# Finer TensorE blocks, one head-sum form, the root's product on GpSimd and an early exponential in a pre-norm attention and gMLP kernel

## The chip, the cores and the metric

The kernel runs on one core of one Trainium2 chip. The metric is device time in microseconds. The kernel before takes 737.69 us, the median of three runs (737.46 to 737.92).

## The reference

The input x has 2048 rows of 1024 features. Two residual blocks follow each other, each behind a layer norm without gain or offset.

```python
def _A_ref(x, wqkv, wo):            # 32 heads of 32
    W, dil = (8, 2)
    q, k, v = split heads of x @ wqkv
    idx = pos[:, None] - arange(W)[None, :] * dil
    logits = einsum('bhsd,bhswd->bhsw', q, k[idx]) * Dh ** -0.5, masked where idx < 0
    o = einsum('bhsw,bhswd->bhsd', softmax(logits), v[idx])
    return o @ wo

def _B_ref(x, w_in, w_sp, b_sp, w_out):   # F = 3584, Fh = 1792
    z = gelu(x @ w_in)
    z1 = z[..., :Fh]; z2 = layernorm(z[..., Fh:])
    g = einsum('ts,bsf->btf', w_sp, z2) + b_sp[None, :, None]
    return (z1 * g) @ w_out

h   = x + _A_ref(layernorm(x), ...)
out = h + _B_ref(layernorm(h), ...)
```

(The lines of `_A_ref` are shortened.) Attention looks at eight positions, two apart, so its logits are eight elementwise products of q with a shifted k, summed over the 32 features of a head. The spatial product with `w_sp` needs z2 of all rows, so it cannot start before the whole first part is through.

## The kernel before

Rows are worked in four chunks of 512 (four tiles of 128 rows). The kernel has two stages.

**The second stage**, from 442.6 us on, is plain: for each chunk the spatial product (L773), bias and gate on VectorE (DVE), and the output projection (L788). The change does not touch it.

**The first stage** is a list of operations that is put in order by a small planner at build time, the class `Order`. Each operation has an engine, an estimated duration, dependencies with a latency (0.1 us unless another is given), a priority (lower first), and slots that it takes or frees: three accumulators of two PSUM banks each ("acc"), one PSUM tile for logits ("L"), two product buffers and two partial-sum buffers. The planner keeps a clock for each engine. It picks the engine whose next operation can start first; among the operations of that engine that can start within 0.02 us of that, the lowest priority goes. It also keeps in mind which function table ScalarE (ACT) has loaded and adds 1.28 us where an operation names another one. The result is the order of instructions in the queues of TensorE (PE), ACT, DVE and GpSimd (POOL); on the chip each engine then works through its queue in that order and waits where data is not there yet. The DMAs issued by SP and POOL are put where the planner's time for them falls.

The operations that the change speaks of:

- `qkv(c)` (L351) projects chunk c to q, k and v: 12 accumulators per chunk, each two halves of eight matmuls of 512 columns (1.727 us planned). `b_z2(c)` (L627) and `b_z1(c)` (L677) are the two halves of the gMLP's input projection, `head(c)` (L554) is the attention's output projection. All of them split an accumulator in two halves, and the second depends on the first with the usual latency. ACT empties the accumulators (L363, L358 for q, k, v; L634 and L683 with gelu), for `head` DVE does it while adding the residual (L563).
- `attention(c)` on DVE: for each of eight window positions a product of q and shifted k for all heads (L407, 128x4096), then one add that halves the eight slices of 512 to four (L411). With `LMODE` 2 a second add halves them again to two (L414); with `LMODE` 4 it stops there. TensorE sums the rest of a head's features with a matmul against a 0/1 matrix of 32 columns (L430): in mode 2 two groups, each for four windows and of 8 matmuls with 512 columns, in mode 4 four groups, each for two windows and of 16 matmuls with 256 columns. Chunks 0 and 1 use mode 2, chunks 2 and 3 mode 4. Then the softmax: maximum and subtraction on DVE (L439, L447), exponential on ACT (L449), sums, reciprocal and product on DVE (L453 to L471), the spread over the features on TensorE (L483) and its copies to SBUF (L488), and eight multiplies and seven adds with v on DVE (L501, L504, L510), which end in the attention output oT of the chunk.
- `batch_rstd` computes mean, variance and reciprocal root for the layer norms of h ("l2", after `head`) and of z2 ("l3", after `b_z2`): four small operations on DVE, the root as a power of -0.5 on GpSimd (L524), then on DVE nb = -mean * rstd (L529). ACT then normalises in place with scale rstd and bias nb (L596 for l2 of chunks 0 to 2, L656 for l3 of chunks 0 to 2). Chunk 3's l2 is done per tile with one column and without nb, and DVE normalises (L580); chunk 3's l3 is normalised on DVE too (L658).

TensorE's queue in the first stage mixes these: `qkv(1..3)` runs beside the attention of chunks 0 and 1, `b_z2` and `b_z1` of chunks 0 to 2 beside the attention of chunks 2 and 3, and `head(c)` comes when oT of chunk c is done. `b_z1(2)` is split around `head(3)`; `b_z2(3)` and `b_z1(3)` end the stage. The transposed, normalised h (hnT) comes by DMA transposes from SP's queue (L586, L601).

Of the kernel before, what the change touches and what calls it, by code (L numbers as in the profile page):

```python
# [20 lines left out]
P = 128  # L21
# [10 lines left out]
NEG = -1.0e9  # L32
NWARM = 14
XRB = 2
LMODE = (2, 2, 4, 4)
LSLACK, BSLACK = 2.0, 2.0
Z2ACT = (4, 4, 4, 0)
LNPRIO = (0, 2.0, 2.5, 4.0)
LAST_COLS = ((0, 512), (512, 768), (768, 1024))

# [84 lines left out]
def kernel(  # L125
# [34 lines left out]
    maskb = csb[0:32, 288:416].rearrange("p (w s) -> p w s", w=W_WIN)  # L160
    eps_t = cpool.tile([P, 1], FP32, name="eps_t")
    V.memset(eps_t[:], EPS)
    nhalf = cpool.tile([P, TPC], FP32, name="nhalf")
    V.memset(nhalf[:], -0.5)
    mv1 = cpool.tile([P, NT, 2], FP32, name="mv1")
# [163 lines left out]
    def qkv(c):  # L329
        for xi in range(3):  # L330
            wv = wsb[xi][:].rearrange("p kt (m dl) -> p kt dl m", dl=DLO)
            for dp in range(DLO // 2):
                key = ("acc", "qkv", c, xi, dp)
                deps = [G.get(("xnT", c))]
                if c == 0 and xi == 0 and dp < 2:
                    def mm(wv=wv, dp=dp):
                        if dp == 0:
                            accs = [new_acc(), new_acc()]
                            G["acc", "qkv", 0, 0, 0], G["acc", "qkv", 0, 0, 1] = accs
                            for kt in range(KT):  # L340
                                for dl in range(4):
                                    T.matmul(accs[dl // 2][:, dl % 2, :], wv[:, kt, dl, :], xnT[0][:, kt, :],  # L342
                                             start=(kt == 0), stop=(kt == KT - 1))
                    last = add("PE", 6.91 if dp == 0 else 0.0, mm, deps, prio=order(), take="acc")
                else:
                    for j in range(2):
                        def mm(j=j, dl=2 * dp + j, wv=wv, key=key):
                            if j == 0:
                                G[key] = new_acc()
                            for kt in range(KT):  # L350
                                T.matmul(G[key][:, j, :], wv[:, kt, dl, :], xnT[c][:, kt, :],  # L351
                                         start=(kt == 0), stop=(kt == KT - 1))
                        last = add("PE", 1.727, mm, deps, prio=order(), take="acc" if j == 0 else None)
                        deps = [last]
                def ev(xi=xi, dp=dp, key=key):
                    if c == 0:
                        off = 0 if xi == 0 else HALO
                        A.copy(att_in[0][xi][:, 2 * dp:2 * dp + 2, off:off + CH], G[key][:])  # L358
                        if xi > 0 and dp == 3:
                            dma(qkv_d[xi][:, :, CH - HALO:CH], att_in[0][xi][:, :, CH:CH + HALO])  # L360
                    else:
                        stg = l1.tile([P, 2, CH], BF16, name="stg", tag="xn", bufs=4)
                        A.copy(stg[:], G[key][:])  # L363
                        dma(qkv_d[xi][:, 2 * dp:2 * dp + 2, c * CH:(c + 1) * CH], stg[:])
# [9 lines left out]
    def attention(c):  # L374
# [66 lines left out]
            st["ssum"] = att.tile([P, 4, P], FP32, name="ssum", tag="ssum")  # L441
        prev = add("DVE", 1.18, mx, lms, prio=3.0, take="prod")
        exps = []
        for hw in range(2):
            ws = slice(4 * hw, 4 * hw + 4)
            def sub(ws=ws):
                V.tensor_tensor(st["sme"][:, 0, ws, :], st["L"][:, ws, :], st["m"][:].unsqueeze(1).to_broadcast([P, 4, P]), op=ALU.subtract)  # L447
            prev = add("DVE", 0.61, sub, [prev], prio=3.0, lat=0.1, free="L" if hw == 1 else None)
            exps.append(add("ACT", 0.6, lambda ws=ws: A.activation(st["sme"][:, 1, ws, :], st["sme"][:, 0, ws, :], ACTF.Exp, scale=SCALE),  # L449
                            [prev], prio=0.0, table="exp"))  # L450
# [62 lines left out]


    def batch_rstd(key, sums, sqs, n, pfx, deps, prio, cols=TPC):
        def a1():
            t = {k: bp.tile([P, cols], FP32, name=pfx + k, tag=pfx + k) for k in ("mean", "msq", "var", "rstd", "nb")}
            G[key] = t
            V.tensor_scalar(t["mean"][:], sums(), 1.0 / n, None, op0=ALU.mult)
            V.tensor_tensor(t["msq"][:], t["mean"][:], t["mean"][:], op=ALU.mult)  # L520
            V.scalar_tensor_tensor(t["var"][:], sqs(), 1.0 / n, t["msq"][:], op0=ALU.mult, op1=ALU.subtract)
            V.tensor_scalar(t["var"][:], t["var"][:], 0.0, EPS, op0=ALU.max, op1=ALU.add)
        s1 = add("DVE", 0.74, a1, deps, prio=prio)
        s2 = add("POOL", 1.05, lambda: nc.gpsimd.tensor_tensor(G[key]["rstd"][:], G[key]["var"][:], nhalf[:, 0:cols], op=ALU.pow), [s1], lat=0.4)  # L524
        if cols < TPC:
            return s2
        def a3():
            t = G[key]
            V.scalar_tensor_tensor(t["nb"][:], t["mean"][:], -1.0, t["rstd"][:], op0=ALU.mult, op1=ALU.mult)  # L529
        return add("DVE", 0.16, a3, [s2], prio=prio)  # L530

    def head(c):
        last = c == NCH - 1
# [5 lines left out]
        for il in range(TPC):  # L539
            i = c * TPC + il  # L540
            deps = [G["avdone", c]]
            for half in range(2):
                def mm(half=half, il=il, i=i):
                    if half == 0:
                        if il == 0:
                            st["hsum"] = bp.tile([P, TPC], FP32, name="hsum", tag="hsum")
                            st["hsq"] = bp.tile([P, TPC], FP32, name="hsq", tag="hsq")
# [1 line left out]
                            for k in range(min(XRB, TPC)):  # L549
                                xr_load(k)  # L550
                        st["acc", il] = new_acc()
                    for dl in range(4 * half, 4 * half + 4):
                        for nh in range(2):
                            T.matmul(st["acc", il][:, nh, :], oTs[c][:, dl, il * P:(il + 1) * P], wo_sb[:, dl, nh * CH:(nh + 1) * CH],  # L554
                                     start=(dl == 0), stop=(dl == DLO - 1))
                def xr_load(k):
                    st["xr", k] = bp.tile([P, D], BF16, name="xr", tag="xr", bufs=XRB)
                    dma(st["xr", k][:], x2d[(c * TPC + k) * P:(c * TPC + k + 1) * P, :])
                m_ = add("PE", 1.727, mm, deps, prio=prio + il * 1e-2 + half * 1e-3, take="acc" if half == 0 else None)
                deps = [m_]  # L560
            def res(il=il, i=i):
                hb = st["hnc"][:, il, :]
                V.scalar_tensor_tensor(hb, st["acc", il][:].rearrange("p a b -> p (a b)"), 1.0, st["xr", il][:],  # L563
# [9 lines left out]
        if last:  # L573
            G["close"] = dma_op(0.0, close_, [G["headmm", c]] + [G["z2n", k, il] for k in range(c) for il in range(TPC)])
            for il in range(TPC):
                rs = batch_rstd(("l2", c, il), lambda il=il: st["hsum"][:, il:il + 1], lambda il=il: st["hsq"][:, il:il + 1],
                                D, f"l2_{il}", [sqd[il]], 0.5, cols=1)
                def nrm(il=il):
                    t = G["l2", c, il]
                    V.tensor_scalar(st["hnc"][:, il, :], st["hnc"][:, il, :], t["mean"][:], t["rstd"][:],  # L580
                                    op0=ALU.subtract, op1=ALU.mult)
                n_ = add("DVE", 0.5, nrm, [rs], prio=0.6)
                def tr(il=il):
                    if il == 0:
# [23 lines left out]
    def b_z2(c):  # L608
        st = {}
        sqd = []  # L610
        for il in range(TPC):
            evs = []
            for hf in range(2):
                wd = win_specs[hf][1]
                deps = [G.get(("hnT", c, il), G["hnT", c]), G["win", hf]]
                for half in range(2):
                    def mm(half=half, hf=hf, il=il, wd=wd):
                        if half == 0:
# [5 lines left out]
                        for kt in range(4 * half, 4 * half + 4):  # L624
                            for n0 in range(0, wd, CH):
                                n1 = min(n0 + CH, wd)
                                T.matmul(accf[:, n0:n1], hnTs[c][:, il, kt, :], wins[hf][:, kt, n0:n1],  # L627
                                         start=(kt == 0), stop=(kt == KT - 1))
                    m_ = add("PE", 1.727 if hf == 0 else 1.3, mm, deps, prio=order(), take="acc" if half == 0 else None)
                    deps = [m_]  # L630
# [19 lines left out]
        for il in range(TPC):  # L650
            i = c * TPC + il
            def nrm(il=il, i=i):
# [2 lines left out]
                if Z2ACT[c] > il:  # L655
                    A.activation(z2[:], st["u", il][:], ACTF.Identity, scale=t["rstd"][:, il:il + 1], bias=t["nb"][:, il:il + 1])  # L656
                else:
                    V.tensor_scalar(z2[:], st["u", il][:], t["mean"][:, il:il + 1], t["rstd"][:, il:il + 1], op0=ALU.subtract, op1=ALU.mult)  # L658
# [8 lines left out]
    def b_z1(c):  # L667
        for fp in range(NF // 2):
            deps = [G["hnT", c], G["win", 2 if fp < 4 else 3]]
            for j in range(2):  # L670
                def mm(j=j, fp=fp):
                    f = 2 * fp + j
                    wt, f0 = (wins[2], f) if f < 8 else (wins[3], f - 8)
                    if j == 0:
                        G["accy", c, fp] = new_acc()
                    for kt in range(KT):
                        T.matmul(G["accy", c, fp][:, j, :].rearrange("p (a b) -> p a b", a=TPC), wt[:, kt, f0 * P:(f0 + 1) * P],  # L677
                                 hnTs[c][:, :, kt, :], start=(kt == 0), stop=(kt == KT - 1))
                m_ = add("PE", 1.727, mm, deps, prio=order(), take="acc" if j == 0 else None)
                deps = [m_]  # L680
            def ev(fp=fp):
                z1s = l1.tile([P, 2, CH], BF16, name="z1s", tag="xn", bufs=4)
                A.activation(z1s[:], G["accy", c, fp][:], ACTF.Gelu_apprx_tanh)  # L683
# [150 lines left out]
```

## Time and profile before

| what | value |
|---|---|
| median of three runs | 737.69 us (737.46 to 737.92) |
| the profiled execution: its own time, its span | 737.65 us, 735.9 us |
| mean granted TensorE clock | 0.998 |
| attention outputs done on DVE, chunk 3 | 368.1 us |
| second stage begins | 442.6 us |
| ACT table loads: at L256, L449, L634, L683 | 1, 3, 1, 2 |
| GpSimd roots: L299, l2, l3, l2 of chunk 3 | 3, 3, 4, 4 |

The span runs from the first to the last instruction of one profiled execution; that execution's own time is 1.75 us longer. A row of a group gives the line, the engine, the operation, its tiles and shapes and its count, then the busy time of the group in us and the mean ns of one, then the idle time of the engine just before such an instruction and what ended it. Matmuls are pipelined, so the mean ns of one (379 for 512 columns) is longer than the spacing of two (0.216 us); a group's busy time counts the overlap once. DVE instructions in a row overlap by 0.08 us. A wait's row names engine, line and tile, what it waited for, and us in total, times and the longest. A row of the stages gives the window, its length, and busy time and instruction count of PE, PE's weight loads, DVE, ACT and POOL, then granted clock, DMA share and GB/s.

### The profile page before, as it was taken

The numbers are of one execution on the slowest core, as the hardware profiler recorded it, in microseconds if no ns is written. First come the engines' busy times: TensorE is split into PE (matmuls) and PEld (weight loads), VectorE is DVE, ScalarE is ACT, GpSimd is POOL, SyncE is SP. The second block draws the span as 40 slices with busy tenths as digits, with TensorE's granted clock in tenths as the row PEclk, the third lists the DMA queues.
The fourth block names the chain that finished last, engine by engine and source line by source line (L and its number), as shares of the span: only waits on it lengthen the run. The fifth ranks groups of instructions, "written<-read, shape, count | busy, mean of one in ns | idle before, by whom it ended". The sixth has DMA issues, their size and how long they took to land.

```text
span 735.9 us, 8608 instructions
## 1 busy us (share of the span) xinstructions
PE 725.7 (99%) x3580; PEld 369.1 (50%) x3580; DVE 416.8 (57%) x431; ACT 219.2 (30%) x267; POOL 50.0 (7%) x59
## 2 busy tenths in 40 slices
PE   7999999999999999999999999999999999999998
PEld 4666665566645444444444544444444444444444
DVE  4899899988999899889940012221232223212322
ACT  4322532534338954696563620000000000000000
POOL 0310200100102100300113000000000000000000
PEclk9999999999999999999999999999999999999999
DMA  9874563485484632370079988135104410020002
GB/s 337 315 242 116 191 184 122 153 231 200 149 324 109 210 113 74 115 227 18 29 229 338 256 243 268 40 95 148 58 29 112 133 57 31 28 86 29 1 15 71
DMA packets 113223, 105.27 MB, mean 143 GB/s; under 512 B 67776, under 2 KB 91744, under 8 KB 113056
## 3 DMA queue, kind: packets, MB, share of 16 engines
q1 hardware_dynamic: 105472, 72.63, 33.0%
q0 software_dynamic: 7280, 31.50, 12.1%
q8 instruction: 28, 0.46, 0.3%
q10 hardware_dynamic: 432, 0.59, 0.2%
q14 instruction: 11, 0.09, 0.0%
HBM read 55.09 MB, written 33.88 MB: 121 GB/s over the span
## 4 chain that ended last, share of the span: by engine, by line
PE 89%; DVE 7%; ACT 1%; POOL 1%; issue 1%; DMA 0%; POOLq 0%; DVEq 0%; ACTq 0%
PE acc L773 26%; PE acc L351 22%; PE acc L788 13%; PE acc L627 10%; PE acc L677 9%; PE acc L554 8%; DVE prod L504 2%; DVE oT L510 2%; PE acc L342 1%; DVE part L411 1%; POOL l3rstd L524 1%; PE L L430 1%; DMA xp<-in_A_x_dram 0%; PE tpa L252 0%; ACT z1s L683 0%
## 5 line engine op out<-in xcount | busy, mean ns | idle before, releaser
L773 PE MATMUL acc<-wspT,z2sb 128*128 128x512 bf16 x896 | 194.0, 379 | 0.0
L773 PEld LDWEIGHTS <-z2sb 128*128 128x128 bf16 x896 | 87.7, 98 | 105.7
L776 DVE TENSOR_TENSOR g<-acc,bB 128x1024 bf16<-128x1024 f32 x28 | 34.3, 1224 | 157.6 <-PE acc L773 133.0
L677 PE MATMUL acc<-hnT,win 128*128 128x512 bf16 x448 | 99.4, 379 | 0.5 <-ACT z1s L683 0.5
L627 PE MATMUL acc<-win,hnT 128*128 128x512 bf16 (+1 forms) x512 | 99.3, 352 | 0.0
L627 PEld LDWEIGHTS <-hnT 128*128 128x128 bf16 x512 | 49.8, 98 | 47.7 <-issue 0.9
L407 DVE TENSOR_TENSOR prod<-qT,kT 128x4096 bf16<-128x4096 bf16 x32 | 72.0, 2284 | 1.6 <-ACT kT L358 1.6
L788 PEld LDWEIGHTS <-zg 128*128 128x128 bf16 x462 | 45.2, 98 | 51.7
L677 PEld LDWEIGHTS <-win 128*128 128x128 bf16 x448 | 43.4, 98 | 52.5 <-issue 1.7
L504 DVE TENSOR_TENSOR prod<-vT,AB 128x4096 bf16<-128x4096 bf16 x28 | 63.8, 2289 | 1.0
L510 DVE TENSOR_TENSOR oT<-oT,prod 128x4096 bf16<-128x4096 bf16 x28 | 64.0, 2284 | 0.1
L363 ACT CAST stg<-acc 128x1024 bf16<-128x1024 f32 x36 | 36.4, 1011 | 78.6 <-PE acc L351 75.5
L788 PE MATMUL acc<-wout_a,zg 128*128 128x512 bf16 (+1 forms) x264 | 58.2, 373 | 0.0
L795 DVE TENSOR_TENSOR ot<-acc,hr 128x1024 bf16<-128x1024 f32 x15 | 18.4, 1224 | 69.4 <-PE acc L788 69.4
L351 PE MATMUL acc<-xnT,wv 128*128 128x512 bf16 x256 | 57.1, 380 | 0.0
L351 PE MATMUL acc<-xnT,wk 128*128 128x512 bf16 x256 | 57.1, 380 | 0.0
L554 PE MATMUL acc<-wo_sb,oT 128*128 128x512 bf16 x256 | 56.3, 379 | 0.7 <-DVE oT L510 0.7
L351 PE MATMUL acc<-xnT,wq 128*128 128x512 bf16 x224 | 49.8, 379 | 0.0
L351 PEld LDWEIGHTS <-wk 128*128 128x128 bf16 x256 | 36.4, 143 | 19.1 <-issue 0.9
L351 PEld LDWEIGHTS <-wv 128*128 128x128 bf16 x256 | 36.4, 143 | 19.1 <-issue 0.9
L788 PE MATMUL acc<-wout_b,zg 128*128 128x512 bf16 (+1 forms) x198 | 44.4, 373 | 0.0
L351 PEld LDWEIGHTS <-wq 128*128 128x128 bf16 x224 | 31.9, 143 | 16.8 <-issue 0.8
(125 smaller groups left out, 489.9 us busy)
## 6 DMA issues: line engine op xcount, KB each, us to landing
qkv_d<-stg SPq DMA_DIRECT2D x36, 256.0 KB, 2.5
z_d<-z1s SPq DMA_DIRECT2D x28, 256.0 KB, 2.6
z1c<-z_d SPq DMA_DIRECT2D x28, 256.0 KB, 2.7
z_d<-u SPq DMA_DIRECT2D x12, 448.0 KB, 2.9
z2sb<-z_d POOLq DMA_DIRECT2D x12, 448.0 KB, 9.2
xr<-in_A_x_dram SPq DMA_DIRECT2D x16, 256.0 KB, 2.8
h_d<-hb SPq DMA_DIRECT2D x16, 256.0 KB, 2.4
win<-in_B_w_in_dram POOLq DMA_DIRECT2D x2, 2048.0 KB, 9.1
```

The lines of the kernel that those rows point to most:

```text
L351: T.matmul(G[key][:, j, :], wv[:, kt, dl, :], xnT[c][:, kt, :], start=(kt == 0), stop=(kt == KT - 1))
L363: A.copy(stg[:], G[key][:])
L407: V.tensor_tensor(st["prod"][:], qT[:], kT[:, :, o:o + CH], op=ALU.mult)
L504: V.tensor_tensor(pvs[w][:], vT[:, :, o:o + CH], abb, op=ALU.mult)
L510: prev = add("DVE", 2.3, lambda w=w: V.tensor_tensor(oTs[c][:], oTs[c][:], pvs[w][:], op=ALU.add), [prev, m_], prio=3.0, lat=0.15, free="p ...
L554: T.matmul(st["acc", il][:, nh, :], oTs[c][:, dl, il * P:(il + 1) * P], wo_sb[:, dl, nh * CH:(nh + 1) * CH], start=(dl == 0), stop=(dl == ...
L627: T.matmul(accf[:, n0:n1], hnTs[c][:, il, kt, :], wins[hf][:, kt, n0:n1], start=(kt == 0), stop=(kt == KT - 1))
L677: T.matmul(G["accy", c, fp][:, j, :].rearrange("p (a b) -> p a b", a=TPC), wt[:, kt, f0 * P:(f0 + 1) * P], hnTs[c][:, :, kt, :], start=(kt ...
L773: T.matmul(acc[:, j, :], z2sb[a][:, f * P:(f + 1) * P], wspT[:, a, :], start=(a == 0), stop=(a == NT - 1))
L776: V.tensor_tensor(g1[:], acc[:], bB[:, c * CH:(c + 1) * CH].unsqueeze(1).to_broadcast([P, 2, CH]), op=ALU.add)
L788: T.matmul(outs, zg[:, f, il * P:(il + 1) * P], wt[:, f0, lo:hi], start=(f == 0), stop=(f == NF - 1))
L795: V.tensor_tensor(ot[:], acc[:].rearrange("p a b -> p (a b)"), hr[:], op=ALU.add)
```

## The change

Four things are changed in the list.

1. `LMODE` is 2 for all chunks, so chunks 2 and 3 get the second add on DVE and two groups of 8 wide head-sum matmuls.
2. The accumulators are worked in four blocks of four matmuls instead of two of eight, planned at 0.863 us each, and a block depends on the one before it with latency 0.
3. `batch_rstd` computes the negative mean; for the batches of four columns nb = nmean * rstd is a second operation on GpSimd right behind the root, and the whole is planned at 1.6 us with a latency of 1.2 us. L580 and L658 add the negative mean instead of subtracting the mean.
4. After the last head-sum matmuls of a chunk a one-element-per-partition exponential of a constant is put on ACT, with priority 0 and the exponential table.

```diff
-LMODE = (2, 2, 4, 4)
+LMODE = (2, 2, 2, 2)
+PIECES = ((0, 0), (0, 4), (1, 0), (1, 4))
...
+    texp = cpool.tile([P, 1], FP32, name="texp")
...
-                    for j in range(2):
-                        def mm(j=j, dl=2 * dp + j, wv=wv, key=key):
-                            if j == 0:
+                    for j, k0 in PIECES:
+                        def mm(j=j, k0=k0, dl=2 * dp + j, wv=wv, key=key):
+                            if j == 0 and k0 == 0:
                                 G[key] = new_acc()
-                            for kt in range(KT):
+                            for kt in range(k0, k0 + 4):
                                 T.matmul(G[key][:, j, :], wv[:, kt, dl, :], xnT[c][:, kt, :],
                                          start=(kt == 0), stop=(kt == KT - 1))
-                        last = add("PE", 1.727, mm, deps, prio=order(), take="acc" if j == 0 else None)
-                        deps = [last]
+                        last = add("PE", 0.863, mm, deps, prio=order(), take="acc" if j == 0 and k0 == 0 else None)
+                        deps = [(last, 0.0)]
...
         exps = []
+        add("ACT", 0.2, lambda: A.activation(texp[:], eps_t[:], ACTF.Exp), lms, prio=0.0, table="exp")
...
-        def a1():
-            t = {k: bp.tile([P, cols], FP32, name=pfx + k, tag=pfx + k) for k in ("mean", "msq", "var", "rstd", "nb")}
+        def moments():
+            t = {k: bp.tile([P, cols], FP32, name=pfx + k, tag=pfx + k) for k in ("nmean", "msq", "var", "rstd", "nb")}
             G[key] = t
-            V.tensor_scalar(t["mean"][:], sums(), 1.0 / n, None, op0=ALU.mult)
+            V.tensor_scalar(t["nmean"][:], sums(), -1.0 / n, None, op0=ALU.mult)
...
-        s2 = add("POOL", 1.05, lambda: nc.gpsimd.tensor_tensor(G[key]["rstd"][:], G[key]["var"][:], nhalf[:, 0:cols], op=ALU.pow), [s1], lat=0.4)
-        if cols < TPC:
-            return s2
-        def a3():
+        s1 = add("DVE", 0.74, moments, deps, prio=prio)
+        def root():
             t = G[key]
-            V.scalar_tensor_tensor(t["nb"][:], t["mean"][:], -1.0, t["rstd"][:], op0=ALU.mult, op1=ALU.mult)
-        return add("DVE", 0.16, a3, [s2], prio=prio)
+            nc.gpsimd.tensor_tensor(t["rstd"][:], t["var"][:], nhalf[:, 0:cols], op=ALU.pow)
+            if cols == TPC:
+                nc.gpsimd.tensor_tensor(t["nb"][:], t["nmean"][:], t["rstd"][:], op=ALU.mult)
+        return add("POOL", 1.05 if cols < TPC else 1.6, root, [s1], lat=0.4 if cols < TPC else 1.2)
...
-            for half in range(2):
-                def mm(half=half, il=il, i=i):
-                    if half == 0:
+            for part in range(4):
+                def mm(part=part, il=il, i=i):
+                    if part == 0:
...
-                    for dl in range(4 * half, 4 * half + 4):
+                    for dl in range(2 * part, 2 * part + 2):
...
-                m_ = add("PE", 1.727, mm, deps, prio=prio + il * 1e-2 + half * 1e-3, take="acc" if half == 0 else None)
-                deps = [m_]
+                m_ = add("PE", 0.863, mm, deps, prio=prio + il * 1e-2 + part * 1e-3, take="acc" if part == 0 else None)
+                deps = [(m_, 0.0)]
```

The same split is made in `b_z2` (two of eight steps at a time, 0.863 or 0.653 us) and in `b_z1` (by `PIECES`).

More of the change, by code (lines that the diff above doesn't have):

```diff
@@ L515, in batch_rstd @@
     def batch_rstd(key, sums, sqs, n, pfx, deps, prio, cols=TPC):
-        def a1():
-            t = {k: bp.tile([P, cols], FP32, name=pfx + k, tag=pfx + k) for k in ("mean", "msq", "var", "rstd", "nb")}
+        def moments():
+            t = {k: bp.tile([P, cols], FP32, name=pfx + k, tag=pfx + k) for k in ("nmean", "msq", "var", "rstd", "nb")}
             G[key] = t
-            V.tensor_scalar(t["mean"][:], sums(), 1.0 / n, None, op0=ALU.mult)
-            V.tensor_tensor(t["msq"][:], t["mean"][:], t["mean"][:], op=ALU.mult)
+            V.tensor_scalar(t["nmean"][:], sums(), -1.0 / n, None, op0=ALU.mult)
+            V.tensor_tensor(t["msq"][:], t["nmean"][:], t["nmean"][:], op=ALU.mult)
             V.scalar_tensor_tensor(t["var"][:], sqs(), 1.0 / n, t["msq"][:], op0=ALU.mult, op1=ALU.subtract)
             V.tensor_scalar(t["var"][:], t["var"][:], 0.0, EPS, op0=ALU.max, op1=ALU.add)
-        s1 = add("DVE", 0.74, a1, deps, prio=prio)
-        s2 = add("POOL", 1.05, lambda: nc.gpsimd.tensor_tensor(G[key]["rstd"][:], G[key]["var"][:], nhalf[:, 0:cols], op=ALU.pow), [s1], lat=0.4)
-        if cols < TPC:
-            return s2
-        def a3():
+        s1 = add("DVE", 0.74, moments, deps, prio=prio)
+        def root():
             t = G[key]
-            V.scalar_tensor_tensor(t["nb"][:], t["mean"][:], -1.0, t["rstd"][:], op0=ALU.mult, op1=ALU.mult)
-        return add("DVE", 0.16, a3, [s2], prio=prio)
+            nc.gpsimd.tensor_tensor(t["rstd"][:], t["var"][:], nhalf[:, 0:cols], op=ALU.pow)
+            if cols == TPC:
+                nc.gpsimd.tensor_tensor(t["nb"][:], t["nmean"][:], t["rstd"][:], op=ALU.mult)
+        return add("POOL", 1.05 if cols < TPC else 1.6, root, [s1], lat=0.4 if cols < TPC else 1.2)
     def head(c):
@@ L579, in nrm @@
                     t = G["l2", c, il]
-                    V.tensor_scalar(st["hnc"][:, il, :], st["hnc"][:, il, :], t["mean"][:], t["rstd"][:],
-                                    op0=ALU.subtract, op1=ALU.mult)
+                    V.tensor_scalar(st["hnc"][:, il, :], st["hnc"][:, il, :], t["nmean"][:], t["rstd"][:],
+                                    op0=ALU.add, op1=ALU.mult)
                 n_ = add("DVE", 0.5, nrm, [rs], prio=0.6)
@@ L615, in b_z2, with mm @@
                 deps = [G.get(("hnT", c, il), G["hnT", c]), G["win", hf]]
-                for half in range(2):
-                    def mm(half=half, hf=hf, il=il, wd=wd):
-                        if half == 0:
+                for part in range(4):
+                    def mm(part=part, hf=hf, il=il, wd=wd):
+                        if part == 0:
                             st["acc"] = G["accz", c, il, hf] = new_acc()
@@ L623, in mm @@
                         accf = G["accz", c, il, hf][:].rearrange("p a b -> p (a b)")
-                        for kt in range(4 * half, 4 * half + 4):
+                        for kt in range(2 * part, 2 * part + 2):
                             for n0 in range(0, wd, CH):
@@ L628, in mm @@
                                          start=(kt == 0), stop=(kt == KT - 1))
-                    m_ = add("PE", 1.727 if hf == 0 else 1.3, mm, deps, prio=order(), take="acc" if half == 0 else None)
-                    deps = [m_]
+                    m_ = add("PE", 0.863 if hf == 0 else 0.653, mm, deps, prio=order(), take="acc" if part == 0 else None)
+                    deps = [(m_, 0.0)]
                 def ev(hf=hf, il=il, wd=wd):
@@ L657, in nrm @@
                 else:
-                    V.tensor_scalar(z2[:], st["u", il][:], t["mean"][:, il:il + 1], t["rstd"][:, il:il + 1], op0=ALU.subtract, op1=ALU.mult)
+                    V.tensor_scalar(z2[:], st["u", il][:], t["nmean"][:, il:il + 1], t["rstd"][:, il:il + 1], op0=ALU.add, op1=ALU.mult)
                 if c < NCH - 1:
@@ L669, in b_z1, with mm @@
             deps = [G["hnT", c], G["win", 2 if fp < 4 else 3]]
-            for j in range(2):
-                def mm(j=j, fp=fp):
+            for j, k0 in PIECES:
+                def mm(j=j, k0=k0, fp=fp):
                     f = 2 * fp + j
                     wt, f0 = (wins[2], f) if f < 8 else (wins[3], f - 8)
-                    if j == 0:
+                    if j == 0 and k0 == 0:
                         G["accy", c, fp] = new_acc()
-                    for kt in range(KT):
+                    for kt in range(k0, k0 + 4):
                         T.matmul(G["accy", c, fp][:, j, :].rearrange("p (a b) -> p a b", a=TPC), wt[:, kt, f0 * P:(f0 + 1) * P],
                                  hnTs[c][:, :, kt, :], start=(kt == 0), stop=(kt == KT - 1))
-                m_ = add("PE", 1.727, mm, deps, prio=order(), take="acc" if j == 0 else None)
-                deps = [m_]
+                m_ = add("PE", 0.863, mm, deps, prio=order(), take="acc" if j == 0 and k0 == 0 else None)
+                deps = [(m_, 0.0)]
             def ev(fp=fp):
```

## The prediction

> **What bounds the kernel now.** I read the page's first part first, then TensorE's waits, the stages, the chain and the timelines of DVE and POOL around the lines that the change touches. Busy time of each engine:
>
> ```profile
> PE 725.7 (99%) x3580; PEld 369.1 (50%) x3580; DVE 416.8 (57%) x431; ACT 219.2 (30%) x267; POOL 50.0 (7%) x59
> ```
>
> TensorE is busy for all but 10.2 of 735.9 us. The list of TensorE's waits says where it stood still (three of its six rows; the other three are in the first 13.3 us, which the change leaves alone), and the stages give the planned part as a whole:
>
> ```profile
> PE L L430 <- DVE part L411: 1.3, 1, 1.3
> ...
> PE acc L554 <- DVE oT L510: 0.7, 1, 0.7
> PE acc L677 <- ACT z1s L683: 0.5, 1, 0.5
> ```
> ```profile
> 13.30:442.60 429.30, 426.77 (x2177) 231.41 (x2178) 335.86 (x331) 210.57 (x253) 49.10 (x54) 1.00 0.59 185
> ```
>
> So between the first projection and the start of the second stage TensorE works 426.8 us and is idle 2.5 us, at a granted clock of 1.00. Time can come from two places only: less TensorE work, or those 2.5 us. DVE is nearly as full up to 368 us and then almost idle. Whether DVE can still push the end is seen in the chain at the last attention:
>
> ```profile
> 365.79 2.29 DVE oT L510
> 368.08 0.05 issue
> 368.13 13.99 PE acc L554 x64
> 382.12 10.36 PE acc L677 x48
> 392.48 1.73 PE acc L627 x8
> ```
>
> TensorE waits 0.7 us for the attention output of chunk 3, projects it (L554), and then has 10.36 us of L677 left that need nothing of chunk 3, before the first L627 of chunk 3. That is the cover for a later DVE: the planner can place those 48 matmuls ahead of the projection.
>
> The rows by form and the timeline give the prices. In the first fence the columns are busy time and mean ns of one; in the second, start and duration, with the idle time before in brackets:
>
> ```profile
> L430 PE MATMUL L<-part,csb 128*32 128x256 bf16 x128 | 5.0, 275 | 1.3 <-DVE part L411 1.3
> L430 PE MATMUL L<-part,csb 128*32 128x512 bf16 x32 | 2.5, 384 | 0.0
> L414 DVE TENSOR_TENSOR part<-prod 128x1024 bf16<-128x1024 bf16 x16 | 10.4, 683 | 0.0
> L449 ACT ACT_TABLE_LOAD x3 | 3.8, 1283 | 0.1
> ```
> ```profile
> 140.30 1.22 DVE L411 TENSOR_TENSOR prod<-prod 128x2048 bf16<-128x2048 bf16 x1
> 142.45 0.16 DVE L529 SCALAR_TENSOR_TENSOR l2nb<-l2mean,l2rstd 128x4 f32<-128x4 f32 x1 [0.93 <-POOL l2rstd L524]
> ```
> ```profile
> 33.09 1.04 POOL L299 TENSOR_TENSOR rstd<-ve,nhalf 128x4 f32<-128x4 f32 x1 [5.15 <-DVE ve L297]
> ...
> 140.48 1.93 POOL L524 TENSOR_TENSOR l2rstd<-l2var,nhalf 128x4 f32<-128x4 f32 x1 [23.64 <-DVE l2var L522]
> ...
> 304.57 2.90 POOL L524 TENSOR_TENSOR l2rstd<-l2var,nhalf 128x4 f32<-128x4 f32 x1 [23.39 <-DVE l2var L522]
> ```
>
> **Two slices in chunks 2 and 3.** Four groups of 16 head-sum matmuls per chunk become two groups of 8, twice as wide. A group of either kind takes 0.55 us in the chain, so TensorE loses 2 chunks x 2 groups x 0.55 = 2.2 us of work. This is on the path, because TensorE is the path. DVE gets one more add per window: 16 x 0.60 us (two L414 in a row span 1.28, one 0.68) = 9.6 us, all before 368 us.
>
> **Blocks of four.** The number of matmuls is unchanged, but the dependency between blocks of one accumulator drops from 0.1 us to zero. In the list of before the second half was 0.1 us late and the next accumulator's first half got in between, so accumulators end in pairs: the residual adds of chunk 3 start at 373.52, 375.25, 380.43 and 382.15, and the evictions (L363) at 178.90, 180.63, 185.81, 187.53. A pair A, B held two of three slots; the fourth accumulator started 8.64 us after A began and A ended at 5.18, a slack of 3.45 us for the eviction. In sequence A ends at 3.45 and the fourth starts at 10.36: slack 6.91 us. I expect this to remove the 0.45 us wait for L683. A finer block also lets the small attention matmuls in earlier: DVE waited 1.52 + 0.98 + 0.72 us for the last L430 of chunks 1 to 3 and 5.4 us for L483. Half a block less (0.43 us) at eight such places is 3.5 us of DVE; the bounds are 0 and 2 x 3.5.
>
> **Root and product on GpSimd.** Seven L529 leave DVE; five of them, up to 368 us, stood in DVE's queue with 0.90 to 0.93 us of idle time before them (three l2, and l3 of chunks 1 and 2), 4.6 us in all, plus 0.1 us each. Behind the waiting L529 stood the next attention multiply. GpSimd gets a second small operation, and ScalarE's normalisation (L596, L656) now waits for that one. The trace has no such product. Its nearest rows are the roots: 0.54 us for one column, 1.04 for four, but 1.93 and 2.90 to 3.00 where a DVE add of 1.22 or multiply of 2.28 us ran; each ends 0.9 us after DVE's operation. Till now DVE stood idle then; after the change its next operation is waiting. Below: DVE never gives way and saves all 5.1 us. Above: GpSimd is let in between, DVE is held 0.9 + 0.5 = 1.4 us per batch, 7.0 us against 4.6, and loses 2.4. I take DVE as unchanged: the root still holds it 0.9 us, and I count the product as hidden by GpSimd's long idle time. The factor nb then reaches ScalarE about 0.5 us to 2.28 + 0.5 = 2.8 us later than before. Cover: the eviction slack of 6.91 us, against one normalisation of 1.87 and an eviction of 1.02 behind it, in all 5.7 us. If that cover were gone, each microsecond late would be one of TensorE. The four single-column roots of chunk 3 get no product. The last l3 batch, at 423 us, gets one that nobody reads; the second stage starts 19 us later.
>
> The Trainium skill ("SBUF — State Buffer", Who interferes with whom) says that a VectorE operation with two SBUF inputs and a GpSimd operation that reads SBUF exclude each other, and the later one blocks until the first is through. That agrees with 1.04 against 2.90 us and speaks against putting a second operation on GpSimd beside a full VectorE. By it the sum would take the upper end, 2.4 us more DVE time, and 2.4 us more TensorE idle if none of it is covered; what happens when both always have the next operation queued neither the page nor this trace says.
>
> **Exponential ahead.** A tiny exponential of 0.2 us (L256 took 202 ns) is placed on ScalarE after the last head sum. Three loads of 1.28 us stand before L449; DVE waited 1.34 and 0.97 us for it in chunks 2 and 3 (0.94 in chunk 1, where no load stood; none in chunk 0). At most about 0.9 us in each of two chunks goes, 1.8 us of DVE. If a gelu eviction slips between the early load and the exponentials, two loads are added instead (2.57 us of ScalarE) and DVE waits some 1.6 us more. That is ScalarE and DVE time with 10.36 us of cover, so I put it at nothing on the path.
>
> **Sum.** DVE up to chunk 3's output: + 9.6 - 3.5 + 0 - 1.8 = about + 4.3 us (from 9.6 + 2.4 + 3.2 = + 15.2 with nothing won back to 9.6 - 7.0 - 5.1 - 1.8 = - 4.3). TensorE reaches the same place 2.2 + 0.45 us sooner, so it needs about 7 us of other work there and has 10.36. After the projection the first transposed tile is due by head start + 3.45 (first accumulator) + 5.1 (residual add at 373.52 to transpose issue at 378.58) + 3.9 to land = 12.4 us, inside the projection's 13.8; so spending the cover opens no second hole. The moved matmuls take three stores of z_d with them, ahead of xr, h_d and the transposes on SP's queue, at about 0.33 us of issue each; the reloads of z2sb on POOL (from 385.8 us) and wspT on SP (401.7) shift with the projection by some 5 us, and are needed at 442.6. DVE's lateness against the planner's order (1.31 + 0.74 us of TensorE waits) I leave as it is, since its cause, the unplanned waits at the roots, is taken as unchanged. The profiled execution took 737.65 us (735.9 span and 1.75 around it; median of the runs 737.69): 737.65 - 2.2 - 0.45 = **735.0 us**. All idle time gone would be 737.65 - 2.2 - 2.5 = 732.9.
>
> **Rivals.** *DVE becomes the bound at the last attention* (0.20). For it: DVE has no idle time to speak of there. Against: the 48 matmuls. With nothing won back DVE is 9.6 us later, TensorE 2.2 + 1.8 sooner: 13.6 - 10.36 = 3.2 us idle, 732.9 + 3.2 = 736.2; with GpSimd's 2.4 us on top 738.6. Between these it is no measurable change.
>
> *GpSimd never gets in, and ScalarE stands* (0.14, the other side). Place: the l2 batches of chunks 0, 1, 2 (140, 224, 304 us), where DVE's two-input operations follow each other without a gap for about 18, 15 and 16 us. If the root or the product waits for the end of such a run, ScalarE stands at L596 that long and evicts nothing; TensorE goes on for 6.91 us and then idles 11 + 8 + 9 = 28 us, 763 us. It decides once the three waits average more than 6.91 + 1.4 = 8.3 us (4.2 us in all, from 735.0 to 739.2). For it: the roots do wait for DVE today. Against: each got in 0.9 us after the end of a single operation, though DVE's queue stood still then.
>
> *The load isn't ahead*, because a gelu eviction takes the table back: likely in one of the chunks 2 and 3, but worth nothing in time, as said; it lies inside the forecast. The last 0.04 is a reordered list that leaves holes that I can't place, slower.
>
> **How the numbers follow.** Forecast 0.62, with its own range 732.9 to 736.2. A measurement of this kernel tells 0.2% (1.5 us) from no change, so faster is below 736.2 and slower above 739.2. Faster 0.62; same 0.20 (DVE-bound); slower 0.14 + 0.04 = 0.18. The forecast and the DVE case reach from 732.9 to 738.6 and hold 0.82; as the slower case begins at 739.2 with its mild end, I take in its first two microseconds: 732.9 to 741.
>
> **What would show it.** Eight L430 groups with 512 columns and TensorE busy near 723.5 us; L414 x32; evictions 3.45 us apart instead of 1.7 and 5.2; L677 ahead of the last L554 and fewer than 48 behind it; no idle time of DVE before its next operation at the roots, and GpSimd's pair ending 1 to 4 us after DVE's variance. It is wrong if TensorE's idle time between 13 and 440 us exceeds 4 us: a wait for L683, L634 or L363 would mean ScalarE stood, one for L411, L414 or L510 that DVE is late.

## The result, and the profile after

The changed kernel takes 772.15 us (median of four runs, 766.04 to 777.84) against 737.68 us before; the ratio is 1.0441 with a 95% interval of 1.0381 to 1.0501. A ratio leaves out executions more than 1.5% above the fastest of the same kernel and a median counts them all, so the two differ where the times scatter (one of four executions is left out here, three of six and one of four in two experiments below). The forecast was 735.0 us, 732.9 to 741. The change is slower by 34 us (33 by the ratio), and by neither of the priced ways.

The profiled execution spans 772.8 us (before 735.9). Its busy times, and TensorE's waits after the first 13 us (engine, line, tile and what it waited for; us in total, times, longest):

```profile
PE 723.6 (94%) x3423; PEld 367.8 (48%) x3484; DVE 426.3 (55%) x440; ACT 224.0 (29%) x273; POOL 52.8 (7%) x66
```
```profile
PE acc L629 <- DMA hnT<-hb: 34.2, 1, 34.2
PE L L432 <- DVE part L416: 3.3, 2, 1.8
...
PE acc L629 <- DVE hb L565: 0.5, 1, 0.5
PE pb L486 <- DVE attn L474: 0.3, 1, 0.3
```

TensorE's busy time fell by 2.1 us. That row does not measure the work alone, as 61 matmuls left no record (3423 against 3484 weight loads) and part of the work ran at a lower clock (below). The head sums' own row, 4.9 us busy in place of 5.0 + 2.5, agrees with the forecast saving of 2.2 us:

```profile
L432 PE MATMUL L<-part,csb 128*32 128x512 bf16 x64 | 4.9, 384 | 3.3 <-DVE part L416 3.3
```

One wait of 34.2 us, for a transposed tile of the last chunk, is new. The chain of work that ended last shows what stood behind it (start, us, what):

```profile
413.44 28.62 SPq L697
442.15 5.47 DMA hnT<-hb
447.67 7.27 PE acc L629 x30
```

L697 (L695 before) is the first load of wspT, the transposed spatial weights. SP's queue around it, first before, then after (start, time in the queue, what it issues):

```profile
387.45 3.97 SPq L586 DMA_TRANSPOSE hnT<-hb  x1
391.52 10.11 SPq L684 DMA_DIRECT2D z_d<-z1s  x3
401.73 11.95 SPq L695 DMA_TRANSPOSE wspT<-in_B_w_sp_dram  x1
```
```profile
396.52 0.53 SPq L686 DMA_DIRECT2D z_d<-z1s  x1
397.15 44.91 SPq L697 DMA_TRANSPOSE wspT<-in_B_w_sp_dram  x1
442.15 3.46 SPq L588 DMA_TRANSPOSE hnT<-hb  x1
```

Before, the last hnT went ahead of wspT. After, wspT goes ahead of it, stays 44.9 us in place of 11.95, and hnT is issued only at 442.15, though its source was ready at 397.1. The load of wspT depends on the last z1 eviction of chunk 2 and on the projection L556; nothing ties it to hnT. The planner now puts 36 of the 48 z1 matmuls ahead of the projection, so that eviction comes just ahead of the last normalised tile in its order, and wspT slipped in.

At the same time GpSimd's reloads of z2sb run (the normalised z2 of chunks 0 to 2, brought back for the second stage). POOL's last four of twelve, after (the bracket is the idle time before, spent waiting for earlier reloads to land):

```profile
402.00 0.54 POOL L738 DMA_DIRECT2D z2sb<-z_d  x1 [0.73 <-DMA z2sb<-z_d]
406.39 0.54 POOL L738 DMA_DIRECT2D z2sb<-z_d  x1 [3.85 <-DMA z2sb<-z_d]
428.89 0.54 POOL L738 DMA_DIRECT2D z2sb<-z_d  x1 [21.96 <-DMA z2sb<-z_d]
430.01 0.54 POOL L738 DMA_DIRECT2D z2sb<-z_d  x1 [0.59 <-DMA z2sb<-z_d]
```

The reloads crawl as well: a median of 31.1 us to land, 9.2 before. In a run below, where most of the reloads follow wspT, wspT lands 12.6 us after issue (49.6 here) and the reloads after a median of 6.4. The stage rows add the clock (window, its length, busy time of PE, PE's weight loads, DVE, ACT, POOL, granted clock, DMA share, GB/s):

```profile
413.00:447.60 34.60, 0.42 (x3) 0.04 (x1) 0.00 (x0) 2.69 (x4) 1.08 (x2) 0.55 1.20 122
447.60:456.00 8.40, 8.28 (x36) 3.92 (x38) 0.00 (x0) 1.81 (x3) 0.90 (x1) 0.83 0.13 25
```

The granted clock falls to 0.55 in the wait and costs, as an estimate, another 0.17 x 8.4 = 1.4 us behind it. From 13.3 to 30 us it was 0.89 in this execution (1.00 in the one of before), 0.11 x 16.7 = 1.8 us. With 1.6 us more of other idle time (4.1 against 2.5) and the forecast 2.2 us less work, 735.9 + 34.2 + 1.4 + 1.8 + 1.6 - 2.2 = 772.7 us, the measured span within 0.1 us. So the loss has its place, 34.2 us of it as one measured wait and the small terms in part as estimates.

### The profile page after: what moved, and what is told of

Read it like the earlier page. It is cut to its first block, busy times and chain, and to the rows that moved or that the text cites. A ratio compares the mean times of both kernels' runs of the same rounds, so it can differ in the third digit from the quotient of the medians.

```text
span 772.8 us, 8374 instructions
## 1 busy us (share of the span) xinstructions
PE 723.6 (94%) x3423; PEld 367.8 (48%) x3484; DVE 426.3 (55%) x440; ACT 224.0 (29%) x273; POOL 52.8 (7%) x66
## 4 chain that ended last, share of the span: by engine, by line
PE 79%; DVE 6%; issue 6%; DMA 5%; SPq 4%; ACT 0%; POOL 0%; DVEq 0%; POOLq 0%
PE acc L775 25%; PE acc L353 13%; PE acc L790 12%; PE acc L679 12%; PE acc L629 10%; PE acc L556 6%; SPq L697 4%; DMA xp<-in_A_x_dram 3%; DVE prod L409 1%; DMA xr<-in_A_x_dram 1%; DVE prod L413 1%; DVE bnst L226 1%; DVE bnst L227 1%; DMA hnT<-hb 1%; DMA xn_d<-xn 1%
## 5 line engine op out<-in xcount | busy, mean ns | idle before, releaser
L629 PE MATMUL acc<-win,hnT 128*128 128x512 bf16 (+1 forms) x501 | 99.5, 355 | 35.3 <-DMA hnT<-hb 34.2
L556 PE MATMUL acc<-wo_sb,oT 128*128 128x512 bf16 x250 | 55.6, 379 | 0.3
L353 PE MATMUL acc<-xnT,wq 128*128 128x512 bf16 x219 | 49.6, 380 | 0.3
L636 ACT ACTIVATE u<-acc 128x1024 bf16<-128x1024 f32 (+1 forms) x32 | 29.2, 914 | 61.2 <-PE acc L629 61.2
## 6 DMA issues: line engine op xcount, KB each, us to landing
z2sb<-z_d POOLq DMA_DIRECT2D x12, 448.0 KB, 31.1
```

## The experiments

Theory: the load of wspT, released early by the moved z1 matmuls, runs beside the reloads of z2sb, and the last hnT is stuck behind or among them. Rivals: the queue's order alone does it; or the parts of the change themselves (two slices, blocks, GpSimd's product) cost the time.

**wspT gated on hnT, all else as changed** (run twice)

```diff
-    dma_op(0.0, wsp0, [G["z1ev", NCH - 2], G["close"]])
+    dma_op(0.0, wsp0, [G["z1ev", NCH - 2], G["close"], G["hnT", NCH - 1]])
```

> The changed kernel with one more dependency: the first load of wspT is placed behind the last transposed tile of chunk 3 (hnT). Theory (SP's queue): wspT, issued at 397.15 us and 44.9 us long in the queue, stood in front of the last hnT, and TensorE's 34.2 us wait is that. Then the wait for hnT goes (under 1 us) and the time falls from 772 to 736 to 743 us; wspT is still slow beside the reloads of z2sb (over 30 us), so a wait for wspT or for a z1s buffer of up to 6 us may come near 440 us. Rival (the stage itself is slower, through DVE's second add or ScalarE behind GpSimd): TensorE's idle time only moves elsewhere and the time stays over 755.

> The changed kernel with wspT behind all hnT once more, one look, since its times went from 743 to 773 us and the profile fell on the shortest. Theory: in a slower execution it is the last hnT that lands late though issued ahead of wspT (its packets share the DMA engines with wspT's and the reloads'), or TensorE waits for wspT or a z1s buffer near 445 us; wspT stays over 30 us in the queue.

Measured: 757.88 us (743.42 to 772.67), ratio 1.0119 (1.0067 to 1.0172); a single further execution 745.0. The forecast of 736 to 743 missed: the right order is not enough. SP's queue in the first profile, and the transfers of the second between 395 and 440 us (count, median us from issue to landing):

```profile
395.84 1.27 SPq L588 DMA_TRANSPOSE hnT<-hb  x1
397.21 24.55 SPq L697 DMA_TRANSPOSE wspT<-in_B_w_sp_dram  x1
```
```profile
wspT<-in_B_w_sp_dram SPq DMA_TRANSPOSE x2, 22.7
hnT<-hb SPq DMA_TRANSPOSE x1, 22.6
```

hnT is issued ahead of wspT and still lands late, 20.9 us after issue in the first profile and 22.6 in the second; TensorE waits 4.7 and 6.1 us for it. Both profiles are of short executions. What the longer ones (up to 772.67) wait for is not shown.

**The reloads on SP's queue, behind wspT, and ahead of it**

```diff
-            dma_w(z2sb[i][:], z2_d[i * P:(i + 1) * P, :])
+            dma(z2sb[i][:], z2_d[i * P:(i + 1) * P, :])
```

The second run has this edit and the gate.

> The changed kernel with the twelve reloads of z2sb issued on SP's queue in place of GpSimd's; wspT stays in front of the last hnT, and ten of the reloads now follow it. Theory with a collision (wspT is slow because z2sb's reloads run beside it): wspT's stay in the queue falls from 44.9 to 7 to 14 us, the last hnT lands near 413 us, TensorE waits 0 to 5 us, 736 to 743 us in all. Rival (queue order alone, the transpose is slow at this place for another reason): wspT stays over 30 us and the time over 760.

> The changed kernel with both edits: wspT behind all hnT, and the twelve reloads of z2sb on SP's queue, so that the queue holds hnT, the reloads, then wspT. If the slow transposes come from running beside the reloads, wspT's stay in the queue is under 15 us here too and hnT lands without delay: no wait for hnT, 735.5 to 737.5. Rival (only the side of the queue matters, not what runs together: reloads from GpSimd's queue are the harm): the same, unless the tail of the reloads overlaps wspT; then wspT stays over 20 us with no cost. Rival (the order hnT before wspT matters little): equal to the run with the reloads behind wspT, 736.8.

Measured: 736.78 us (736.02 to 739.19), ratio 0.9985 (0.9970 to 0.9999), with wspT still ahead of the last hnT; 737.2 us, ratio 0.9995 (0.9983 to 1.0007), with the order mended too. SP's queue of the first:

```profile
395.18 10.49 SPq L697 DMA_TRANSPOSE wspT<-in_B_w_sp_dram  x1
405.77 1.27 SPq L588 DMA_TRANSPOSE hnT<-hb  x1
407.08 5.71 SPq L738 DMA_DIRECT2D z2sb<-z_d  x10
```

The order that looked fatal costs nothing once the reloads no longer run beside wspT: 10.49 us in place of 44.91, hnT is out at 405.77, and TensorE has no wait for it. The rival of order alone falls. In the second run the tail of the reloads overlaps wspT, which stays 14.4 us, at no cost.

**The collision made in the kernel before**

```diff
-    dma_op(0.0, wsp0, [G["z1ev", NCH - 2], G["close"]])
+    dma_op(0.0, wsp0, [G["close"]])
```

The second run has the reloads on SP's queue as well.

> The kernel before with one dependency taken away: the first load of wspT no longer waits for the last z1 eviction of chunk 2, only for the attention's projection of chunk 3. It then stands in SP's queue ahead of two transposed tiles and starts near 386 us, when GpSimd's reloads of z2sb start. Nothing of the change is in this kernel. Theory (collision of wspT and the reloads): wspT stays in the queue over 25 us, TensorE waits 15 to 40 us for hnT, 755 to 780 us. Rival (the parts of the change themselves cost the time): within 2 us of 737.7.

> The same early wspT in the kernel before, ahead of the same two transposed tiles, with the reloads of z2sb on SP's queue behind it, so that they cannot run beside it. Theory (it is the collision, not the queue order): wspT takes 7 to 12 us, the two tiles land before they are needed (about 400 and 406 us), no TensorE wait for hnT over 2 us, 736.5 to 740. Rival (queue order alone): as slow as the run without this edit, over 755.

Measured: 754.61 us (747.92 to 766.55), ratio 1.0179 (1.0135 to 1.0224); with the reloads on SP 737.85, ratio 1.0004 (0.9992 to 1.0015). TensorE's wait and SP's queue in the first, then SP's queue in the second:

```profile
PE acc L627 <- DMA hnT<-hb: 14.5, 1, 14.5
```
```profile
382.07 11.34 SPq L695 DMA_TRANSPOSE wspT<-in_B_w_sp_dram  x1
393.50 0.53 SPq L565 DMA_DIRECT2D h_d<-hb  x1
394.13 1.29 SPq L684 DMA_DIRECT2D z_d<-z1s  x1
395.50 17.85 SPq L586 DMA_TRANSPOSE hnT<-hb  x1
```
```profile
382.14 9.08 SPq L695 DMA_TRANSPOSE wspT<-in_B_w_sp_dram  x1
391.31 0.53 SPq L565 DMA_DIRECT2D h_d<-hb  x1
391.94 0.38 SPq L684 DMA_DIRECT2D z_d<-z1s  x1
392.41 1.28 SPq L586 DMA_TRANSPOSE hnT<-hb  x1
```

One dependency brings 13 us by the ratio (17 in the profiled execution) into a kernel that has no part of the change, and taking the reloads out of the way takes it back. The time and the wait are a little under what I expected (755 to 780 us, 15 to 40), and the form differs: wspT leaves the queue after 11.3 us but lands only 30.3 us after issue, and the next transpose, a small hnT, is held 17.85 us.

**One part alone**

```diff
-LMODE = (2, 2, 4, 4)
+LMODE = (2, 2, 2, 2)
```

> The kernel before with two slices per head sum in all chunks and nothing else. In its queue on SP wspT stands in front of two transposed tiles (chunk 3, tiles 2 and 3). Theory: the second add delays the attention output, the planner pulls z1 of chunk 2 ahead of it, and wspT with it: TensorE waits 25 to 45 us for hnT, 760 to 785 us. Rival (blocks of four or the GpSimd product is the cause): within 3 us of 737.7.

The other run makes only the split into blocks of four with latency 0 (its diff is part of the change's).

> The kernel before with blocks of four matmuls at latency 0 and nothing else; wspT stays behind all hnT. Accumulators end 3.45 us apart, the 0.45 us wait for L683 goes, DVE gets its head sums up to 0.43 us sooner per place. Theory: 735.5 to 737.7, no wait for hnT. Rival (the split itself costs TensorE time): TensorE's busy time over 727 or a time over 739.

Measured: 764.73 us (758.4 to 765.87), ratio 1.0337 (1.0302 to 1.0373), for the two slices; 737.39, ratio 0.9985 (0.9973 to 0.9997), for the blocks. TensorE's wait and SP's queue with two slices alone:

```profile
PE acc L627 <- DMA hnT<-hb: 28.9, 3, 26.5
```
```profile
394.04 29.80 SPq L695 DMA_TRANSPOSE wspT<-in_B_w_sp_dram  x1
423.93 0.53 SPq L565 DMA_DIRECT2D h_d<-hb  x1
424.55 8.19 SPq L586 DMA_TRANSPOSE hnT<-hb  x2
```

So the two slices, which bring DVE 9.6 us more in chunks 2 and 3, move the z1 matmuls and with them wspT. The blocks alone leave it behind hnT and gain 0.15%; there wspT stays 20.1 us beside the reloads and the last hnT lands 15.8 us after issue, both at no cost.

**What is left with the collision gone**

All three have the gate, the reloads on SP and three buffers for xr; the second and third undo one part each.

```diff
-XRB = 2
+XRB = 3
...
-LMODE = (2, 2, 2, 2)
+LMODE = (2, 2, 4, 4)
...
-                nc.gpsimd.tensor_tensor(t["nb"][:], t["nmean"][:], t["rstd"][:], op=ALU.mult)
+            V.scalar_tensor_tensor(t["nb"][:], t["mean"][:], -1.0, t["rstd"][:], op0=ALU.mult, op1=ALU.mult)
```

> As the run with both edits, with three buffers for the residual rows xr in place of two. Tiles of the attention's output projection now end 3.45 us apart; DVE waited 5.5 us for the third xr in chunk 1, and TensorE 3.3 us for the head sums of chunk 2 behind it. Theory (that is the TensorE idle time that ate the gain): the waits for L416 fall under 1.5 us and the time to 733.5 to 735.5. Rival (they come from DVE's longer attention): unchanged waits, 736 to 737.

> As the run with three xr buffers, with four slices per head sum back in chunks 2 and 3. By the prices of the rows TensorE's head sums take 2.2 us more and DVE's attention 9.6 us less. If the two slices are worth their 2.2 us on the path, this is 2.2 us slower than that run (736 to 738); if DVE's 9.6 us cost as much through waits, equal within 0.7 us; if more, faster.

> As the run with three xr buffers, with the product nb back on DVE (L529's form, behind the root). DVE waits 0.9 us at each of five batches again, 4.6 us in all, and is 5 us later at the last attention. If GpSimd's product frees DVE and holds it nowhere, DVE's idle time at these places is the whole difference and TensorE's waits for DVE grow by 0 to 4 us: 0 to 4 us slower. If the product on GpSimd held DVE or ScalarE, it is faster.

Measured: three buffers 734.13 us, ratio 0.9950 (0.9932 to 0.9969); four slices back 735.35, ratio 0.9972 (0.9961 to 0.9984); product back on DVE 732.99, ratio 0.9939 (0.9922 to 0.9956), the fastest of all. The line that cost 3.3 us, in the run with three buffers:

```profile
PE L L432 <- DVE part L416: 0.5, 1, 0.5
```

The third buffer takes 3 us away, as its wait said. The two slices are worth 1.2 us by the medians, of 2.2 us of work, but these two intervals overlap slightly, so their size is not settled. The product on GpSimd is worth nothing: without it the kernel is 1.1 us faster, but the two intervals overlap too, so no more than "no gain" is shown.

> The kernel before with only the side edits of the fastest run: reloads of z2sb on SP's queue ahead of wspT, and three buffers for xr. Its TensorE idle time between 13 and 442 us was 2.5 us and none of it was for xr or hnT, so I expect no gain: 736.5 to 738.5. If it falls to 734 or lower, the fastest run's gain is not the change's.

Measured: 737.64, ratio 0.9994 (0.9984 to 1.0004). The side edits by themselves do nothing for the kernel before; the 0.6% of the fastest run comes from the rest of the change, freed of its collision and without GpSimd's product.

## Why the prediction was wrong

**The step that failed** is the sentence on the moved matmuls' company: "the reloads of z2sb on POOL (from 385.8 us) and wspT on SP (401.7) shift with the projection by some 5 us, and are needed at 442.6", and with it "spending the cover opens no second hole". The reloads do shift with the projection (385.8 to 396.6 us). wspT does not (401.7 to 397.2): its release is the last z1 eviction of chunk 2, which belongs to the very matmuls that I moved ahead of the projection. Relative to hnT it moves forward, not back. In place of the step the runs showed wspT ahead of the last hnT, 44.9 us in the queue, and TensorE waiting 34.2 us; the same collision made in the kernel before costs 13 us. I followed the moved matmuls' own stores through SP's queue, but not the transfer that waited for them. And I asked of wspT only when it is needed, not what it runs beside: the row of before (11.95 us beside the tail of the reloads) was taken as its price, while it stays 20 to 45 us in the changed kernel and its variants where more of the reloads run beside it.

A second step failed with it: "3.9 to land" is the first transposed tile's, and I checked only that one against the projection. The last one was the one that came late, and the profile of before already said so. Its last two hnT, issued at 385.50 and 387.45 us as the reloads began, landed as follows:

```profile
DMA to landing us min/median/max: 5.7/12.3/19.0
```

Of the last one's 19.0 us, 14.3 had passed before wspT was issued, so beside the reloads and the z1 stores a small transpose is slow without wspT too. Before, this cost TensorE nothing. With 36 matmuls moved ahead of the projection it does: where wspT is gated and the reloads stay on GpSimd's queue, the wait of 4.7 to 6.1 us is left. In the runs with the reloads on SP's queue every hnT of chunk 3 lands within 4.9 us.

The sign of being wrong did come: 38.3 us of TensorE idle time in the first stage against the limit of 4. But the wait behind it is for a DMA, and none of the waits that I had named. In the prediction's own terms the result belongs to the last 0.04, a reordered list whose holes it did not place.

**The rivals.** *DVE becomes the bound*: no; TensorE does not wait for oT. *GpSimd never gets in*: no. POOL's root and product of the l2 batch of chunk 1, one product beside a DVE subtraction that reads PSUM, and DVE's multiplies beside the first two:

```profile
225.57 1.40 POOL L529 TENSOR_TENSOR l2rstd<-l2var,nhalf 128x4 f32<-128x4 f32 x1 [22.65 <-DVE l2var L525]
227.05 1.29 POOL L531 TENSOR_TENSOR l2nb<-l2nmean,l2rstd 128x4 f32<-128x4 f32 x1
...
248.15 0.20 POOL L531 TENSOR_TENSOR l3nb<-l3nmean,l3rstd 128x4 f32<-128x4 f32 x1
```
```profile
226.00 4.48 DVE L409 TENSOR_TENSOR prod<-qT,kT 128x4096 bf16<-128x4096 bf16 x2
```

GpSimd waits for the end of DVE's operation in flight (1.29 us against 0.20), then gets in. DVE, with its next operation queued, loses nothing: two multiplies take 4.48 us as elsewhere. That is the lower end of my bracket; the upper end, the rule of the Trainium skill ("SBUF — State Buffer", Who interferes with whom) read as blocking DVE too, did not show in these rows. *The load isn't ahead*: as expected in chunk 3, where a gelu eviction took the table back. ScalarE, after:

```profile
328.91 1.28 ACT L446 ACT_TABLE_LOAD   x1
...
331.95 1.28 ACT L685 ACT_TABLE_LOAD   x1 [1.55 <-issue]
...
334.29 1.28 ACT L452 ACT_TABLE_LOAD   x1
...
336.75 1.28 ACT L636 ACT_TABLE_LOAD   x1
```

Four loads where there were two; DVE waited 3.6 us for the exponential against 0.97. TensorE has no wait there.

**The terms.** Two slices, 2.2 us of TensorE work: right in size as work (64 head-sum matmuls with 512 columns, DVE's L416 32 times), worth 1.2 us in a comparison that noise does not settle. The wait for the z1 eviction (0.45 us): gone in every run with blocks of four. The accumulators end 3.45 us apart (residual adds at 382.35, 385.81, 389.26, 392.71). What I missed in that step is who must keep up: xr (the residual rows) has two buffers, and its third load now came 5.5 us late in chunk 1:

```profile
219.02 1.23 DVE L565 SCALAR_TENSOR_TENSOR hb<-acc,xr 128x1024 bf16<-128x1024 f32 x1 [5.54 <-DMA xr<-in_A_x_dram]
```

Behind it TensorE waited 3.3 us for the head sums, which ate the forecast gain: with the collision gone the kernel is at 736.8, not 735.0. With a third buffer, which was no part of the change, it is at 734.1, and at 733.0 without GpSimd's product; both lie inside the forecast's own range of 732.9 to 736.2. DVE's output of chunk 3 came 9.3 us later than before (377.4), not 4.3; 1.8 us of it is the slow start by the estimate above, and the 5.5 us for xr are more than the rest of the difference. The cover held it: 12 of the 48 matmuls were left behind the projection.

## What to carry to other kernels

When a planner may move work, list not only what that work needs but every transfer that waits for it, and look at what that transfer will then run beside. A load that is "needed much later" can still do harm if it starts early: tie a large transposing load to the end of the transfers that the critical path waits for, rather than to whatever happened to finish last. Here that alone was not enough (743 to 773 us): the large reloads that ran at the same time had to be moved out of the way too. For each transfer that the critical path waits for, read the landing time of the last tile and not of the first. A finer spacing of results needs its inputs at the finer spacing too; count the buffers of every operand of the consumer.

## What the runs showed of the hardware

A transposing load of 2 MB from SP's queue stays 7.3 to 8.7 us in the queue for the later chunks (16.1 once, in the run with the product back on DVE). The first load stays 11.95, 20.1, 24.6, 29.6, 29.8 and 44.9 us where GpSimd's reloads (12 x 448 KB) run beside it, and 9.1 to 17.0 us where the reloads are on SP's queue. The early one in the kernel before stays 11.3 us and lands after 30.3. The reloads' median landing is 9.2 us before and 31.1 after, and 10.0 to 16.0 in the other runs on GpSimd's queue. The slowest small hnT of chunk 3 (256 KB) lands 15.8 to 23.8 us after issue in five of the seven profiles with the reloads on GpSimd's queue (5.5 and 7.2 in the other two, where it is issued as they end), and within 4.9 us in all seven with the reloads on SP's queue. Over the 44.9 us the DMA engines moved a mean of 152 GB/s at a DMA share of 1.19, against 314 GB/s at 1.18 in the 12 us of before: they are busy, but not with bytes. The Trainium skill ("DMA: Bandwidth & Descriptors", Rules for kernel authors) says that a transpose next to ordinary DMAs needs nothing; that is said of its data, and these runs show that its time needs care. Why they slow each other, and whether it takes GpSimd's queue or only the same time, is open: in the runs without the harm the reloads were both on SP's queue and largely out of the way.

The granted clock between 13.3 and 30 us was 1.00 in the profile of before and in most others, but 0.87 to 0.89 in the changed kernel's and in three of the last variants', which costs 1.8 us by the estimate above; what decides it was not tried.
